# Attention with a mixture of experts: the product with wi in TensorE's two row halves, one step later; first ids ahead of the weights; the third batch's gates earlier

## The chip, the cores and the metric

The kernel runs on one core of a Trainium2 chip. The metric is the device time of one execution in microseconds (us). Each comparison takes the median of several executions. One further execution is profiled: the hardware profiler records every instruction of TensorE (PE, its weight loads as PEld), VectorE (DVE), ScalarE (ACT), GpSimd (POOL) and SyncE (SP, which here issues DMAs), every DMA, and the clock granted to TensorE.

## The reference

Causal attention over 4 batches, 12 heads, 448 positions, 64 elements a head; its output, rows of 12 x 64 = 768 elements, goes through a layer of 8 experts of which each row takes the one with the largest gate logit.

```python
scores = scale * np.matmul(q, k.transpose(0, 1, 3, 2))     # causal mask on top
attn = np.exp(scores - np.max(scores, axis=-1, keepdims=True))
attn = attn / (np.sum(attn, axis=-1, keepdims=True) + 1e-09)
x = np.matmul(attn, v)                                     # then rows of B*S, columns of H*D
...
logits = x @ w_gate
expert_idx = np.argmax(logits, axis=1)
probs = np.exp(logits - logits.max(-1, keepdims=True))
probs /= probs.sum(-1, keepdims=True) + 1e-09
gate_w = probs[np.arange(N), expert_idx]
for e in range(E):
    mask = expert_idx == e
    out[mask] = gate_w[mask, None] * (np.maximum(x[mask] @ w1[e], 0.0) @ w2[e])
```

## The kernel before

**Pairs and steps.** The attention works on 24 pairs of heads (`NP`), six to a batch (`NPB`). The 448 positions are four chunks of 112 (`C`). The order of the instructions on every engine is the order in which the code is written. `step(p)` lays pair p+1's scores beside pair p's transposes and pair p-1's values, and is called for p from -1 to 22; a list written out by hand takes the place of step 23 (the tail).

**One step.** `scores(n, c)` (n = p+1) multiplies chunk c of the queries with the keys up to it, for the pair's two heads, whose 64 elements lie in partitions 0 to 63 and 64 to 127: two matmuls of 64 rows, into two PSUM banks. VectorE masks and takes the row maximum (L137), ScalarE takes exp and its row sum (L141). `transposes(p, j)`, j from 0 to 4, turns four blocks of 112 x 112 each into one PSUM bank (L160); ScalarE copies them to `pt` (L167), but j = 1 is copied by VectorE (L165). `values(p-1, kc)` multiplies by v (L178); its result, transposed, is copied to `xt` by VectorE (L184), which takes the reciprocal row sums `rs` too (L187, L188).

**The product with wi.** `back(p-1, i)` for i = 0 and 1 closes the step: two chunks of `xt` each are the stationary operand, and `wi` the moving one, 128 rows of 144 columns. `wi` holds, for each pair and for each of the two heads, an identity of 64 columns and that head's rows of `w_gate`, 8 columns; the other head's rows are zero. So one product turns x back into rows and gives the head's part of the logits. VectorE scales both by `rs` into `x` (112 x 256) and `lgp` (112 x 32) (L206, twice each per `back`); after i = 1 SyncE writes x to the rows `xd` in DRAM (L211).

**PSUM.** The tag "pst" of the pool `ps_t` has three banks. The five transposes of a step, the two psb tiles of `back`, and now and then the rank's tile take these three in turn; a tile's first matmul waits for the reader of the tile that had the bank before.

**Routing.** After a batch's sixth pair has gone through `back`, `route(b)` is put on the list `todo`. It is a generator: `drip()` runs it up to its next `yield`, one piece after each transposes of a step (from pair 18 on, after each scores too). Its pieces: `choose` (POOL adds the logits' parts up, VectorE finds the maximum and the one-hot choice), ScalarE's exp, `rank` (four matmuls with triangular and all-one matrices count each row's place, L325 and L326, into a bank of "pst"), `places` (row numbers; POOL scatters the rows' numbers into the tables `idtab` in DRAM with four indirect DMAs, L345), and `gates` (the gate's value, written to `xd`, L320). For the third batch (b = 2) `early_slots` comes between places and gates: it finds, from the three batches counted so far, the experts of the first three slots of 128 rows. There SyncE reads slot 0's expert number, issues two loads of raw weights (`load_raw`, L565, 768 KB each), then slot 0's four id columns (`load_ids`, L572, from `idtab`), then two further weight loads. The last four weight loads, POOL's `merge_ids`, and its `gather` of the rows (L586) stand at the end of `route(2)`.

**The tail and the experts.** The tail runs the last pair's transposes and values between the first weights' splits (`split_parts`, ScalarE L622 and VectorE L628) and turns the first gathered slot (`x_turn`, L657); then the slots of the experts run one after another (L697 on).

## Time and profile before

| | us |
|---|---|
| median of three executions | 533.37 (529.67 to 534.95) |
| the profiled execution | 535.47, of which the profile's span is 533.6 |
| TensorE busy in the span | 506.9 (95%) |
| VectorE, ScalarE busy | 308.8 and 309.8 (58% each) |
| POOL busy | 119.5 (22%) |

The attention takes the span's first 206 us, the experts the rest. The page of the profile gives shares of whole runs; the timeline gives each engine's groups of equal instructions with their start, their length and, in brackets, how long the engine sat idle before them and what ended that; a table of windows gives any stretch's busy times and the granted clock, as a share of full speed. A group's length runs from its first start to its last end. A matmul in float32 is recorded as two rows, each with its weight load.

### The profile page before, as it was taken

The numbers are of one execution on the slowest core, as the hardware profiler recorded it, in microseconds if no ns is written. First come the engines' busy times: TensorE is split into PE (matmuls) and PEld (weight loads), VectorE is DVE, ScalarE is ACT, GpSimd is POOL, SyncE is SP. The second block draws the span as 40 slices with busy tenths as digits, with TensorE's granted clock in tenths as the row PEclk, the third lists the DMA queues.
The fourth block names the chain that finished last, engine by engine and source line by source line (L and its number), as shares of the span: only waits on it lengthen the run. The fifth ranks groups of instructions, "written<-read, shape, count | busy, mean of one in ns | idle before, by whom it ended". The sixth has DMA issues, their size and how long they took to land. (4 is left out here: it accounts for less than half of the span.)

```text
span 533.6 us, 10959 instructions
## 1 busy us (share of the span) xinstructions
PE 506.9 (95%) x3114; PEld 408.0 (76%) x3114; DVE 308.8 (58%) x826; ACT 309.8 (58%) x692; POOL 119.5 (22%) x199
## 2 busy tenths in 40 slices
PE   8999999999998898999999999999999999989991
PEld 5666665675675666898899889988998899878871
DVE  4777776776766687731113635648437213795590
ACT  6878767777776674521224636457455424974660
POOL 1000122013014327131120311214323110333213
PEclk9999999999999798999999999999999999999997
DMA  8544425533635759011157486486673169967720
GB/s 208 137 132 133 140 83 87 173 98 116 134 100 101 133 145 380 10 32 33 51 164 281 134 269 215 141 282 216 225 244 121 51 173 316 328 210 248 247 88 17
DMA packets 56537, 85.33 MB, mean 160 GB/s; under 512 B 16906, under 2 KB 28426, under 8 KB 56464
## 3 DMA queue, kind: packets, MB, share of 16 engines
q1 hardware_dynamic: 53072, 73.42, 47.1%
q0 software_dynamic: 3392, 11.08, 5.5%
q8 instruction: 28, 0.46, 0.4%
q14 instruction: 45, 0.37, 0.4%
HBM read 137.68 MB, written 12.88 MB: 282 GB/s over the span
## 5 line engine op out<-in xcount | busy, mean ns | idle before, releaser
L628 DVE TENSOR_TENSOR lo<-raw,hi 128x1536 fp32r<-128x1536 f32 x64 | 110.2, 1755 | 30.8 <-ACT hi L622 21.5
L141 ACT ACTIVATE s<-s,nm 112x112 f32<-112x112 f32 (+1 forms) x192 | 99.2, 518 | 46.6 <-DVE nm L137 43.2
L622 ACT CAST hi<-raw 128x1536 fp32r<-128x1536 f32 x64 | 92.9, 1484 | 10.8 <-PE y L782 7.9
L137 DVE CUSTOM_DVE_ANT_0 s<-ps,cs 112x112 f32<-112x112 f32 (+1 forms) x192 | 75.4, 446 | 21.9 <-PE ps L134 20.3
L697 PE MATMUL l<-hi,xh 128*128 128x512 f32 x216 | 87.3, 404 | 0.0
L686 ACT COPY hs<-l 128x512 f32<-128x512 f32 x36 | 21.1, 586 | 92.6 <-PE l L684 92.4
L787 PE MATMUL y<-lo,hh 128*128 128x384 f32 x280 | 72.7, 341 | 0.1
L702 PE MATMUL l<-lo,xh 128*128 128x512 f32 x180 | 72.0, 400 | 0.6
L782 PE MATMUL y<-hi,hh 128*128 128x384 f32 x250 | 64.6, 340 | 0.4
L134 PE MATMUL ps<-qk 64*112 64x112 f32 (+3 forms) x384 | 60.4, 432 | 0.9 <-DVE nm L137 0.6
L718 DVE SCALAR_TENSOR_TENSOR hl<-hT,hh 128x512 fp32r<-128x512 f32 x28 | 19.3, 689 | 68.2 <-ACT hh L715 38.0
L160 PE MATMUL pst<-cs,s 112*112 112x112 f32 x480 | 57.9, 268 | 0.5 <-ACT pt L167 0.5
L160 PEld LDWEIGHTS pst<-cs,s 112*112 112x112 f32 x480 | 46.9, 136 | 11.7 <-issue 6.4
L178 PE MATMUL psx<-pt,v 112*64 112x448 f32 (+3 forms) x384 | 50.6, 406 | 0.0
L787 PEld LDWEIGHTS y<-lo,hh 128*128 128x128 f32 x280 | 49.8, 189 | 0.4 <-issue 0.4
L178 PEld LDWEIGHTS psx<-pt,v 112*64 112x64 f32 x384 | 25.5, 137 | 30.8 <-issue 20.9
L697 PEld LDWEIGHTS l<-hi,xh 128*128 128x128 f32 x216 | 41.1, 190 | 8.6 <-issue 0.2
L715 ACT ACTIVATE hh<-hT 128x512 fp32r<-128x512 f32 x36 | 21.8, 605 | 43.9 <-PE hT L712 37.8
L167 ACT COPY pt<-pst 112x448 f32<-112x448 f32 x95 | 45.6, 525 | 2.4 <-PE pst L160 2.3
L782 PEld LDWEIGHTS y<-hi,hh 128*128 128x128 f32 x250 | 44.7, 188 | 1.1 <-issue 0.7
L659 DVE TENSOR_TENSOR xl<-xT,xh 128x384 fp32r<-128x384 f32 x36 | 18.4, 553 | 45.8 <-ACT xh L658 45.7
L134 PEld LDWEIGHTS ps<-qk 64*112 64x112 f32 x384 | 28.7, 181 | 19.3 <-issue 9.8
(147 smaller groups left out, 686.5 us busy)
## 6 DMA issues: line engine op xcount, KB each, us to landing
raw<-in_w SPq DMA_DIRECT2D x144, 768.0 KB
qk<-in_qk SPq DMA_DIRECT2D x23, 448.0 KB
v<-in_v SPq DMA_DIRECT2D x24, 224.0 KB
xd<-x SPq DMA_DIRECT2D x24, 224.0 KB
idc<-idtab SPq DMA_DIRECT2D x72, 0.5 KB
qk<-in_qk SPq DMA_DIRECT2D x2, 224.0 KB
wi<-in_wi SPq DMA_DIRECT2D x1, 432.0 KB
xg<-xd,idx POOLq DMA_INDIRECT x18
```

The source lines that it names most:

```text
L134: nc.tensor.matmul(ps[:, :n], t[o, 0, c * C:(c + 1) * C], t[o, 1, :n], start=True, stop=True)
L137: nc.vector.tensor_tensor_reduce(out=s[:, :n], in0=ps[:, :n], in1=cs[:C, O_MASK + S - n:O_MASK + S], scale=-0.125, scalar=3.0e38, op0=ALU. ...
L141: nc.scalar.activation(s[:, :n], s[:, :n], ACTF.Exp, bias=nm[:, h, c:c + 1], scale=-1.0, accum_out=sm[:, c, h:h + 1],)
L160: nc.tensor.transpose(ps[:, i * C:(i + 1) * C], pr_t[p, h, qc][:, kc * C:(kc + 1) * C], ident[:C, :C])
L167: nc.scalar.copy(dst, ps)
L178: nc.tensor.matmul(ps[D * h:D * (h + 1), kc * C:], v[:, kc, h, :], pt[:, o:o + n], start=(kc == 0), stop=(kc == NCH - 1),)
L622: nc.scalar.copy(parts[u][0], flat(u))
L628: nc.vector.tensor_tensor(out=lo, in0=flat(u), in1=hi.bitcast(F32), op=ALU.subtract)
L697: nc.tensor.matmul(ps, xh[:, k], wh[:, i], start=(k == 0), stop=False)
L702: nc.tensor.matmul(ps, xh[:, k], wl[:, i], start=False, stop=False)
L782: nc.tensor.matmul(y_ps[s][d], hi[:, c], wh[:, i, o], start=(h == 0 and c == 0), stop=False)
L787: nc.tensor.matmul(y_ps[s][d], hi[:, c], wl[:, i, o], start=False, stop=(h == 1 and c == 3))
```

## The change

`wi` loses its zeros: 128 x 6 x 72, each head's identity and gate columns in that head's own 64 partitions (216 KB instead of 432). `back(p)` is called once a pair: eight matmuls of 64 rows and 72 columns, head 0's rows and head 1's in turn, into two banks, one for each head. VectorE still runs four instructions, now by head instead of by pair of chunks. In `step(p)` it is called for p-2 instead of p-1, behind `scores(n, 0)` and `scores(n, 1)` and ahead of the transposes. `route(b)` is put on its list right behind that call. For the first three batches `gates` runs ahead of `rank` instead of last. In `early_slots` slot 0's ids come ahead of all eight weight loads.

```diff
-    wi = const.tile([128, NPB, 2 * HW], F32, name="wi")
+    wi = const.tile([128, NPB, HW], F32, name="wi")
...
-    def back(p, i):
+    def back(p):
...
-        ps = ps_t.tile([C, 2, 2 * HW], F32, tag="pst", name="psb")
-        for j in range(2):
-            c = 2 * i + j
-            nc.tensor.matmul(ps[:, j], xt[:, c * C:(c + 1) * C], wi[:, pr], start=True, stop=True)
-        src = ps.rearrange("p c (h w) -> p c h w", w=HW)
-        for dst, lo, n in ((X[p], 0, D), (LG[b][:, :, 2 * pr:2 * pr + 2], D, E)):
-            nc.vector.tensor_tensor(
-                out=dst[:, 2 * i:2 * i + 2], in0=src[:, :, :, lo:lo + n],
-                in1=rs[:, 2 * i:2 * i + 2, :].unsqueeze(3).to_broadcast([C, 2, 2, n]), op=ALU.mult,
-            )
...
+        both = [ps_t.tile([C, NCH, HW], F32, tag="pst", name="psb") for _ in range(2)]
+        for c in range(NCH):
+            for h, ps in enumerate(both):
+                o = slice(D * h, D * (h + 1))
+                nc.tensor.matmul(ps[:, c], xt[o, c * C:(c + 1) * C], wi[o, pr], start=True, stop=True)
+        for h, ps in enumerate(both):
+            for dst, lo, n in ((X[p][:, :, h], 0, D), (LG[b][:, :, 2 * pr + h], D, E)):
+                nc.vector.tensor_tensor(
+                    out=dst, in0=ps[:, :, lo:lo + n],
+                    in1=rs[:, :, h:h + 1].to_broadcast([C, NCH, n]), op=ALU.mult,
+                )
...
         yield
+        if b < B - 1:
+            yield from gates(b)
         yield
         rank(b)
...
-        yield from gates(b)
+        if b == B - 1:
+            yield from gates(b)
         if b == B - 2:
             for i in range(1, EARLY):
                 load_regs(i)
                 load_ids(i)
-            for u in range(4, 8):
-                load_raw(0, u)
...
         pos = [
-            (scores, n, 0), (scores, n, 1), (transposes, p, 0), (transposes, p, 1), (transposes, p, 2), (scores, n, 3),
+            (scores, n, 0), (scores, n, 1), (back, p - 2), (transposes, p, 0), (transposes, p, 1), (transposes, p, 2), (scores, n, 3),
             (scores, n, 2), *((values, p - 1, kc) for kc in range(NCH)), (transposes, p, 3), (transposes, p, 4),
-            (back, p - 1, 0), (back, p - 1, 1),
         ]
         for f, *a in pos:
             f(*a)
+            if f is back and p - 1 > NPB - 1 and (p - 1) % NPB == 0:
+                todo.append(route((p - 2) // NPB))
...
         regs[0] = nc.sync.value_load(tab0[0:1, 0:1], min_val=0, max_val=E - 1), None, None
-        for i in range(2):
-            load_raw(0, i)
         load_regs(0)
         load_ids(0)
-        for i in range(2, 4):
+        for i in range(8):
             load_raw(0, i)
...
-            if p >= 1 and (p - 1) % NPB == NPB - 1:
-                todo.append(route((p - 1) // NPB))
...
         for f, *a in [
-            (transposes, p, 0), (transposes, p, 1), (split_parts, 0, (0,), ("low",)), (transposes, p, 2),
+            (back, p - 2), (transposes, p, 0), (transposes, p, 1), (split_parts, 0, (0,), ("low",)), (transposes, p, 2),
             (split_parts, 0, (1,), ("high",)), *((values, p - 1, kc) for kc in range(NCH)),
-            (transposes, p, 3), (split_parts, 0, (1,), ("low",)), (transposes, p, 4), (back, p - 1, 0), (back, p - 1, 1),
-            *((values, p, kc) for kc in range(NCH)), (x_turn, 0), (back, p, 0), (back, p, 1),
+            (transposes, p, 3), (split_parts, 0, (1,), ("low",)), (transposes, p, 4), (back, p - 1),
+            *((values, p, kc) for kc in range(NCH)), (x_turn, 0), (back, p),
```

The first place is TensorE at the turn from one step to the next, before the change: the four matmuls of `back` (L203), the four of scores (L134), and the first transposes (L160), with the engines that each waits for (the numbers behind a name tell tiles apart).

```order
L203 MATMUL psb_477<-wi_70,xt_460 112x144 [waits DVE_49,Activation_49]
L203 MATMUL psb_477<-wi_70,xt_460 112x144
L203 MATMUL psb_482<-wi_70,xt_460 112x144 [waits Activation_49]
L203 MATMUL psb_482<-wi_70,xt_460 112x144
L134 MATMUL ps_495<-qk_272 112x112 [waits DMAHW5_49]
L134 MATMUL ps_496<-qk_272 112x112
L134 MATMUL ps_505<-qk_272 112x224
L134 MATMUL ps_506<-qk_272 112x224
L160 MATMUL pst_516<-cs_69,s_396 112x112 [waits Activation_49]
```

After the change, the same place: the scores stand where `back` stood, and `back` behind them.

```order
L134 MATMUL ps_487<-qk_272 112x112 [waits DMAHW5_49,DVE_49]
L134 MATMUL ps_488<-qk_272 112x112 [waits DVE_49]
L134 MATMUL ps_497<-qk_272 112x224 [waits DVE_49]
L134 MATMUL ps_498<-qk_272 112x224 [waits DVE_49]
L203 MATMUL psb_508<-wi_70,xt_464 112x72 [waits DVE_49,Activation_49]
L203 MATMUL psb_509<-wi_70,xt_464 112x72 [waits Activation_49]
L203 MATMUL psb_508<-wi_70,xt_464 112x72
L203 MATMUL psb_509<-wi_70,xt_464 112x72
```

What moved: the product with wi has gone from ahead of the scores to behind them, as eight matmuls of half width.

The second place is the next few rows on TensorE before the change: T0's last transposes, then T1 (tile pst_522) and T2 (pst_528).

```order
L160 MATMUL pst_516<-cs_69,s_435 112x112
L160 MATMUL pst_522<-cs_69,s_406 112x112 [waits DVE_49,PE_49]
L160 MATMUL pst_522<-cs_69,s_445 112x112
L160 MATMUL pst_522<-cs_69,s_435 112x112
L160 MATMUL pst_522<-cs_69,s_445 112x112
L160 MATMUL pst_528<-cs_69,s_435 112x112 [waits DVE_49,PE_49]
L160 MATMUL pst_528<-cs_69,s_435 112x112
```

After the change, T1 is tile pst_530 and T2 pst_536.

```order
L160 MATMUL pst_524<-cs_69,s_439 112x112
L160 MATMUL pst_530<-cs_69,s_393 112x112 [waits DVE_49,PE_49]
L160 MATMUL pst_530<-cs_69,s_449 112x112
L160 MATMUL pst_530<-cs_69,s_439 112x112
L160 MATMUL pst_530<-cs_69,s_449 112x112
L160 MATMUL pst_536<-cs_69,s_439 112x112 [waits Activation_49]
L160 MATMUL pst_536<-cs_69,s_439 112x112
```

What moved: T1 waits for VectorE as before, T2 for Activation (ScalarE) where it waited for VectorE; this stands so in every step that has a `back` in it.

The third place is SyncE's queue behind the third batch, before the change: reading slot 0's expert number (L420), raw weights (L565), and slot 0's ids (L572); DMASW is the queue of POOL's scatters.

```order
L420 TENSOR_LOAD tab_112 [waits DVE_49]
L420 ISA x2
L565 ISA
L565 DMA raw_116<-in_w 128x3x512 [waits DMAHW7_49]
L565 ISA
L565 DMA raw_117<-in_w 128x3x512 [waits DMAHW0_49]
L532 TENSOR_LOAD tab_112 [waits DVE_49]
L532 ISA x2
L572 REGISTER_ALU
L572 DMA idc<-idtab_73 128x1 [waits DMAHW1_49,DMASW0_49]
L572 REGISTER_ALU
L572 DMA idc<-idtab_74 128x1 [waits DMAHW2_49,DMASW1_49]
```

After the change, the gates' row (L322) stands ahead of them, and the ids ahead of the weights.

```order
L322 DMA xd<-pre 112x4x8 [waits DMAHW6_49,DVE_49]
L210 DMA xd<-x 112x4x128 [waits DMAHW7_49,DVE_49]
L422 TENSOR_LOAD tab_112 [waits DVE_49]
L422 ISA x2
L532 TENSOR_LOAD tab_112 [waits DVE_49]
L532 ISA x2
L572 REGISTER_ALU
L572 DMA idc<-idtab_73 128x1 [waits DMAHW0_49,DMASW0_49]
L572 REGISTER_ALU
L572 DMA idc<-idtab_74 128x1 [waits DMAHW1_49,DMASW1_49]
L572 REGISTER_ALU
L572 DMA idc<-idtab_75 128x1 [waits DMAHW2_49,DMASW2_49]
```

What moved: `pre` has gone from behind the ids and four of the weights to the front, and the weights from both sides of the ids to behind them.

## Rows read from the trace of the kernel before

**Rows 1.** TensorE's steps in windows: length, busy time (instructions) of each engine, PEclk, DMA share, GB/s
```profile
68.68:86.29 17.61, 16.01 (x126) 10.64 (x125) 11.90 (x54) 12.31 (x41) 5.50 (x12) 1.00 0.36 104
101.53:109.15 7.62, 7.62 (x61) 5.08 (x61) 5.63 (x26) 6.06 (x20) 0.00 (x0) 1.00 0.45 120
116.77:134.27 17.50, 16.01 (x126) 10.63 (x125) 12.09 (x54) 12.32 (x41) 5.40 (x12) 1.00 0.39 106
157.23:186.77 29.54, 26.41 (x185) 17.98 (x184) 20.35 (x101) 18.50 (x61) 11.41 (x41) 0.88 0.66 117
```

**Rows 2.** Timeline of one undisturbed step: start us, us, engine, line, operation, xcount
```profile
101.15 0.42 DVE L206 TENSOR_TENSOR x<-psb,rs 112x256 f32<-112x256 f32 x1 [0.58 <-PE psb L203]
101.49 0.18 DVE L206 TENSOR_TENSOR lgp<-psb,rs 112x32 f32<-112x32 f32 x1
...
101.53 0.83 PE L134 MATMUL ps<-qk 64*112 64x112 f32 x8
...
102.12 0.28 DVE L137 CUSTOM_DVE_ANT_0 s<-ps,cs 112x112 f32<-112x112 f32 x1
...
102.29 1.36 PE L160 MATMUL pst<-cs,s 112*112 112x112 f32 x12
...
102.44 0.39 ACT L141 ACTIVATE s<-s,nm 112x112 f32<-112x112 f32 x1 [1.34 <-DVE nm L137]
...
103.14 0.08 DVE L137 DVE_READ_ACCUMULATOR2_ANT nm<- 112x1 f32 x1
...
103.58 1.57 PE L134 MATMUL ps<-qk 64*112 64x448 f32 x8
...
104.13 0.94 ACT L167 COPY pt<-pst 112x448 f32<-112x448 f32 x2
...
108.02 1.21 PE L203 MATMUL psb<-wi,xt 128*112 128x144 f32 x8
```

**Rows 3.** Timeline of TensorE in the first batch's rank; idle time before and its releaser in brackets
```profile
71.30 0.36 PE L325 MATMUL rank<-base,cs 112*112 112x40 f32 x2 [0.49 <-DVE pt L165]
71.49 0.36 PE L326 MATMUL rank<-oh,cs 112*112 112x32 f32 x2
71.78 0.63 PE L134 MATMUL ps<-qk 64*112 64x448 f32 x2
```

**Rows 4.** Timeline of TensorE, first two score multiplies of the undisturbed step alone
```profile
101.53 0.45 PE L134 MATMUL ps<-qk 64*112 64x112 f32 x4
```

**Rows 5.** Timeline of TensorE at three waits: step 1, first and third batch's transitions
```profile
14.47 0.80 PE L134 MATMUL ps<-qk 64*112 64x112 f32 x7 [0.33 <-DMA qk<-in_qk]
...
85.15 0.71 PE L203 MATMUL psb<-wi,xt 128*112 128x144 f32 x4 [0.87 <-DVE rs L187]
...
175.04 2.23 PE L203 MATMUL psb<-wi,xt 128*112 128x144 f32 x8 [2.40 <-DVE rs L187]
```

**Rows 6.** Windows behind two stalls, columns as in group 1
```profile
175.04:182.00 6.96, 6.96 (x32) 5.44 (x34) 4.42 (x25) 3.32 (x12) 1.68 (x10) 0.54 0.93 139
205.90:209.20 3.30, 3.30 (x11) 2.73 (x11) 2.80 (x6) 3.30 (x3) 2.32 (x2) 0.57 1.01 387
```

**Rows 7.** Timeline of SyncE's DMA issues behind the third batch
```profile
170.61 1.45 SPq L565 DMA_DIRECT2D raw<-in_w  x2
175.91 9.65 SPq L572 DMA_DIRECT2D idc<-idtab  x4
185.76 0.96 SPq L565 DMA_DIRECT2D raw<-in_w  x2
...
187.34 1.59 SPq L320 DMA_DIRECT2D xd<-pre  x1
```

**Rows 8.** Timeline of GpSimd (POOL): last scatter, and the first slot's gather
```profile
170.17 0.93 POOL L345 DMA_INDIRECT idtab<-ids_c,rowi  x1 [0.30 <-issue]
...
197.27 1.38 POOL L586 DMA_INDIRECT xg<-xd,idx  x1 [7.87 <-DMA idc<-idtab]
```

**Rows 9.** Timeline of TensorE at the first expert's transposes
```profile
203.76 0.87 PE L657 MATMUL xT<-cs,xg 128*128 128x128 f32 x6 [1.67 <-DMA xg<-xd,idx]
```

More of the change, by code (lines that the diff above doesn't have):

```diff
@@ L193, in back @@
         b, pr = divmod(p, NPB)
-        if i == 0:
-            X[p] = x_p.tile([C, NCH, 2, D], F32, name="x")
-            if pr == 0:
-                LG[b] = small.tile([C, NCH, H, E], F32, tag="lgp", name="lgp")
+        X[p] = x_p.tile([C, NCH, 2, D], F32, name="x")
+        if pr == 0:
+            LG[b] = small.tile([C, NCH, H, E], F32, tag="lgp", name="lgp")
         xt = xts_t[p]
         rs = st[p][2]
-        ps = ps_t.tile([C, 2, 2 * HW], F32, tag="pst", name="psb")
-        for j in range(2):
-            c = 2 * i + j
-            nc.tensor.matmul(ps[:, j], xt[:, c * C:(c + 1) * C], wi[:, pr], start=True, stop=True)
-        src = ps.rearrange("p c (h w) -> p c h w", w=HW)
-        for dst, lo, n in ((X[p], 0, D), (LG[b][:, :, 2 * pr:2 * pr + 2], D, E)):
-            nc.vector.tensor_tensor(
-                out=dst[:, 2 * i:2 * i + 2], in0=src[:, :, :, lo:lo + n],
-                in1=rs[:, 2 * i:2 * i + 2, :].unsqueeze(3).to_broadcast([C, 2, 2, n]), op=ALU.mult,
-            )
-        if i == 1:
-            nc.sync.dma_start(
-                xd[b * S:(b + 1) * S, 128 * pr:128 * (pr + 1)].rearrange("(c p) f -> p c f", p=C),
-                X[p].rearrange("p c h d -> p c (h d)"),
-            )
+        both = [ps_t.tile([C, NCH, HW], F32, tag="pst", name="psb") for _ in range(2)]
[9 more added lines that the diff above has]
+                )
+        nc.sync.dma_start(
+            xd[b * S:(b + 1) * S, 128 * pr:128 * (pr + 1)].rearrange("(c p) f -> p c f", p=C),
+            X[p].rearrange("p c h d -> p c (h d)"),
+        )
     todo = []
@@ L317, in gates @@
         V.tensor_scalar_add(g["sm"], g["sm"], 1e-9)
-        yield
+        if b == B - 1:
+            yield
         V.reciprocal(g["pre"], g["sm"].unsqueeze(2).to_broadcast([C, NCH, E]))
@@ L990, in layout @@
     vv = v.reshape(NP, 2, NCH, C, D).transpose(0, 3, 2, 1, 4)
-    wi = np.zeros((128, NPB, 2 * HW), np.float32)
+    wi = np.zeros((128, NPB, HW), np.float32)
     g = moe_w_gate.reshape(NPB, 2, D, E)
     for h in range(2):
-        wi[h * D:(h + 1) * D, :, h * HW:h * HW + D] = np.eye(D, dtype=np.float32)[:, None, :]
-        wi[h * D:(h + 1) * D, :, h * HW + D:(h + 1) * HW] = g[:, h].transpose(1, 0, 2)
+        wi[h * D:(h + 1) * D, :, :D] = np.eye(D, dtype=np.float32)[:, None, :]
+        wi[h * D:(h + 1) * D, :, D:] = g[:, h].transpose(1, 0, 2)
     return {
```

## The prediction

> **What bounds the kernel now.** I read the profile's busy table first: TensorE is busy almost all the time, so the question is only where it waits and how long each step of the attention takes. Then I cut the span into windows, each step from its first score multiply (scores, S) to the next one's [rows 1]: an undisturbed step takes 7.62 us and TensorE is busy for all of it. Two steps after a batch end take 17.61 and 17.50 us instead of 15.24, the three steps after the third batch 29.54 instead of 22.86. These extras, 2.37 + 2.26 + 6.68 = 11.3 us, together with a stall before the mixture of experts, are what a reordering can win. The mixture of experts behind them is untouched by the diff.
>
> Next comes the timeline of one undisturbed step [rows 2]. Read it as one ring: first scores S0+S1 at 101.53, first three transposes T0 to T2 at 102.29, last scores S3, S2 at 103.58, values, T3 and T4, then the product with wi (B) at 108.02; the next S0 at 109.15 ends the window. So S0 to S3 is 2.05 us, S3 to B 4.44, B to S0 1.13; the sum is 7.62.
>
> **Ring of the transposes: the change's price.** B leaves its place, so S0 stands where B stood, 4.44 us behind S3 (4.45, since a turn from full to half rows lies there either way). B now lies between S1 and T0. Its 144 columns become 72, its rows 64, and two halves are to run side by side. No row shows that form. Bounds: the score rows have halves side by side with 112 weight columns, and rank, with only 40 and 32 moving columns, still starts two passes every 0.19 us [rows 3], so 0.095 a pass. Below, half of B's column time, 8 x 0.06 = 0.5; above, sixteen passes one after another, 16 x 0.095 = 1.5. I take 8 x 0.095 = 0.77, since the rank rows are nearest.
>
> What decides is not that figure. B now takes two of the three PSUM banks at the step's front, and the order shows what T1 and T2 then wait for: T1 the VectorE's reading of B's first half, T2 Activation, whose latest instruction of that kind is its copy of T0. Before, both waited for VectorE alone, which was long done. That T2 takes over T0's bank follows from that wait: B's halves and T1 are read by VectorE. Behind T2 stands all of TensorE's queue, and ScalarE's later exps wait for S3. The scores' own new wait for VectorE costs nothing: B in the same place waited for VectorE's later sums.
>
> Worked out from S0's start as 0, with durations of [rows 2]. S0 ends at 0.45 [rows 4]; the max starts at 0.49 (no evacuation of B before it on VectorE any more); the first exp 0.32 later, as 102.12 to 102.44; the four exps take 104.13 - 102.44 = 1.69, so the copy of T0 starts at 2.50. Two copies take 0.94, so one is over 0.5 later, at 3.00, and T2 starts at 3.05. T0 to S3 took 1.29, that is twelve passes of 0.095 and 0.15 around; T2 to S3 is then four passes and 0.15, 0.53. S3 starts at 3.58 instead of 2.05. The step is 3.58 + 4.45 = 8.03 us, 0.41 longer. T1's wait is swallowed in it: the four maxes end at 0.49 + 1.10, x and lgp of the first half follow in 0.34 + 0.18, so T1 starts at about 2.3. With that wait alone S3 would start at 2.3 + 8 x 0.095 + 0.15 = 3.21 and the step be 7.66.
>
> Bounds: if the copy of T0 comes as late as it does now (104.13 + 0.5 is 3.10 behind S0), the step is 8.13; if T2 is not held, 7.66. I take 8.03: the order shows the wait and the chain of exps is a row. It holds in the 21 steps that have a B and scores: 21 x 0.41 = **+8.6 us**. ScalarE's busy time is 6.06 and VectorE's 5.63 of a step [rows 1]: not their sum but the place in the queue holds T2.
>
> The Trainium skill, "TensorEngine Tiling (Array Packing)", section "Performance Considerations", says that tiling speeds up TensorE but not the evacuation of PSUM, which may become the bottleneck. Taken as a sum of evacuation, that rule would cost nothing here, 6.06 being under 7.62; taken as a wait for one copy it is the 8.6 us.
>
> **Start and end of the ring.** The step that had a B first loses it (-1.13), and the wait of 0.33 for qk behind the larger wi falls [rows 5]: **-1.45**. The last product comes into the tail instead: 0.77 and two turns of rows of about 0.1: **+1.0**. Two further products in the tail are cheaper, 8 x (0.121 - 0.095) each, where 0.121 is B's step from 108.02 to 109.15 less 0.16 around it, over eight: **-0.4**.
>
> **Transitions of batches one and two.** Of their extras, rank itself is 0.48 from its first pass to S3 and VectorE wakes it late by 0.49 [rows 3]; B waits 0.87 for a reciprocal sum while the indirect scatters run [rows 5]. Moved between transposes, rank costs four passes, 0.4, without its wait. B is no longer where the scatters land, but other TensorE instructions are; between nothing and 0.87 of that wait, and what the choosing chain takes from VectorE, I take 0.6. So 1.0 a transition, 2.0 instead of 4.63: **-2.6**. The gates moved ahead of rank are three small VectorE instructions, hidden by VectorE's idle 2 us a step.
>
> **Third batch.** B waits 2.40 us, until 175.04 [rows 5]; from there 6.96 us run at a granted clock of 0.54 [rows 6], the lower of the two levels for nearly all of it, 6.96 x 0.46 = 3.2 us lost, and the rest are rank and its wait. Two weight loads are issued at 170.61, right behind the last scatter at 170.17, and run beside the wait [rows 7, 8]. Now no weight is issued before the ids, which wait for the scatters. I take half of the 2.40, no fall of the clock, and rank: 1.6 instead of 6.68: **-5.1**.
>
> **First gather.** SyncE issues the first slot's ids from 175.91, for 9.65 us, and the gates' rows only at 187.34, behind raw weights [rows 7]; the gather on POOL comes at 197.27 after 7.87 us of waiting, and TensorE waits 1.67 us for its rows at 203.76 [rows 8, 9]; then 3.30 us run at 0.57, costing 1.4 [rows 6]. With gates and ids ahead, the gather is issued at about 190 (197.27 less its wait is 189.4) and, at the present 6.5 us from 197.27 to 203.76, lands by 196.5, six before it is needed: **-1.67** and **-1.4**. Its cover: these six us. Of the weights, third and fourth are issued behind the ids at 185.76 already now [rows 7]; the first two move in front of them there, so each comes two loads later, hidden by the 18 us up to 203.76. If that cover went, ScalarE's split and the first expert multiply would wait for them.
>
> **Sum:** 8.6 - 1.45 + 1.0 - 0.4 - 2.6 - 5.1 - 1.67 - 1.4 = -3.0 us. The profiled execution took 535.47 (its span of 533.6 and 1.9 around it), so 532.4; the runs shown have their median 2.1 lower, 533.37, so **530.4**.
>
> **Rivals.**
> *Third batch's stall stays* (whatever instruction stands there waits, and the clock falls after it): the other 1.2 and 3.2 come back, 534.8. For it: the wait is put on a reciprocal that should be long done, so its cause isn't seen. Against: weights no longer run there, and transitions without weights waited 0.87.
> *The gather is still late* (scatters land late, ids too): 1.67 + 1.4 back, 533.5. Against: six us of cover.
> *T2 is not held*: step 7.66, 21 x 0.37 = 7.8 less, 522.6. For it: only an order, no trace, shows the wait. Against: that order, and exps which cannot come earlier.
> *Slower: the clock falls in the lengthened steps.* TensorE would idle about 0.7 us in every one of 21 steps. Both falls in the rows came behind an idle stretch, of 2.40 and 1.67. A fall costs 3.2 or 1.4; from three of the larger kind the change is slower, 530.4 + 9.6 = 540.0. Against: transition steps with waits of 0.87, and 0.49 together with others, kept a clock of 1.00 [rows 1].
> *Slower: the halves don't run side by side*, so the change doesn't do what it says: B takes 1.5, T0 comes 0.77 later and is done at 2.8, its copy at 3.35, S3 starts at 3.93, the step is 8.38: 21 x 0.35 = 7.4 and three products in the tail 2.3 more, 540.1. Against: S3 and S2 in halves take 1.57 for eight rows of 448 and 336 columns; at B's 0.121 per 144 columns one after another they would take 2.6.
> The Trainium skill, "TensorE: Matmul & The Clock Gate", section "LDWEIGHTS (loading the stationary operand)", says that a weight load takes its columns over 1.2 ns, whatever its rows: an estimate of 93 ns for 112 columns, by which halving the rows wins nothing unless both halves load at once. The trace agrees on the 93 (0.095 in rank), and the score rows show loads at once.
>
> **How the numbers follow.** Forecast 0.47, third batch's stall 0.20, late gather 0.13, T2 not held 0.10, clock falls 0.06, halves in turn 0.04. Forecast's own range: half a unit of each taken middle, 527 to 533. From 524.5 to 537.5 leaves out the last three, 0.20. About 1% is what a measurement tells from no change, 528.0 to 538.7: faster are T2 not held and the lower third of the forecast, 0.10 + 0.17; slower the last two, less what they share with a gain, 0.08; the rest, 0.65, is within.
>
> **What would show it.** Step cut as above at 8.0; waits of T1 for VectorE and of T2 for ScalarE's copy, some 0.3 to 0.4 each, in 21 steps; S3 at 3.6 behind S0; B of 0.8 behind S1; TensorE's clock 1.00 behind the third batch's last product, gather issued before 192, no wait of the first expert's transposes. It is wrong if steps stay near 7.6, if a stall of over 2 us stands behind the third batch, or if the clock leaves 1.00 inside the steps.

## The result, and the profile after

The changed kernel takes 539.04 us (median of 4, 538.27 to 539.83) against 532.54 us of the kernel before, measured beside it: 1.011 times the time, 95% interval 1.006 to 1.016. Repeated on another chip it took 536.35 against 529.92, 1.0155 (1.009 to 1.022). It is slower; 530.4 had been forecast, with 537.5 as the range's upper end.

The first view is the windows of the profile after, cut as in [rows 1] at each step's first score multiply: the first batch's transition, an undisturbed step, the second batch's transition, the three steps behind the third batch, the last of these alone, the stretch from there to the first expert's multiply, and the rest.

```profile
70.24:86.76 16.52, 15.66 (x141) 10.37 (x141) 11.79 (x54) 12.55 (x42) 5.81 (x13) 1.00 0.51 89
103.04:111.18 8.14, 7.65 (x69) 5.01 (x69) 5.54 (x25) 6.16 (x21) 0.00 (x0) 1.00 0.66 209
119.31:135.84 16.53, 15.67 (x141) 10.37 (x141) 11.85 (x54) 12.56 (x42) 5.63 (x13) 1.00 0.51 90
160.26:189.32 29.06, 25.67 (x209) 16.11 (x208) 19.39 (x98) 18.08 (x59) 8.31 (x25) 0.94 0.23 52
177.59:189.32 11.73, 9.78 (x69) 5.72 (x68) 6.72 (x39) 5.63 (x18) 1.99 (x8) 0.85 0.16 6
189.32:209.97 20.65, 19.27 (x175) 13.30 (x174) 15.27 (x48) 13.87 (x34) 4.60 (x20) 1.00 0.93 334
209.97:536.40 326.43, 308.99 (x1652) 276.52 (x1650) 162.74 (x202) 158.40 (x205) 87.36 (x113) 0.99 0.52 172
```

An undisturbed step is 8.14 us instead of 7.62. The timeline of one such step shows where (columns as in [rows 2]):

```profile
103.04 0.83 PE L134 MATMUL ps<-qk 64*112 64x112 f32 x8
103.63 0.27 DVE L137 CUSTOM_DVE_ANT_0 s<-ps,cs 112x112 f32<-112x112 f32 x1 [0.45 <-PE ps L134]
103.70 0.92 PE L203 MATMUL psb<-wi,xt 64*112 64x72 f32 x16
103.95 0.39 ACT L141 ACTIVATE s<-s,nm 112x112 f32<-112x112 f32 x1 [0.22 <-DVE nm L137]
...
104.55 0.59 PE L160 MATMUL pst<-cs,s 112*112 112x112 f32 x4
...
105.32 0.56 PE L160 MATMUL pst<-cs,s 112*112 112x112 f32 x4 [0.18 <-DVE lgp L206]
...
105.64 0.51 ACT L167 COPY pt<-pst 112x448 f32<-112x448 f32 x1
...
106.20 0.60 PE L160 MATMUL pst<-cs,s 112*112 112x112 f32 x4 [0.31 <-ACT pt L167]
```

The product runs in 0.85 us, from 103.70 to T0 at 104.55, so its halves do lie side by side. Then T1 waits for VectorE's `lgp` and T2 for ScalarE's copy of T0, which starts at 105.64 behind the four exps. T2 starts 3.16 us behind S0. The two waits, 0.18 and 0.31 us, are nearly all of the 0.52 us that the step has gained; TensorE's busy time in it is 7.65 us against 7.62. The table of waits sums over the whole run (us in total, times, longest); the single row below them is before's, where the first wait was 0.5 us in one instance and the second was not there:

```profile
PE pst L160 <- ACT pt L167: 6.9, 22, 0.5
PE pst L160 <- DVE lgp L206: 3.8, 19, 0.7
PE xT L657 <- DMA xg<-xd,idx: 2.7, 2, 1.7
```

```profile
PE pst L160 <- ACT pt L167: 0.5, 1, 0.5
```

The first slot's gather is now in time, but the second slot's is not. The timelines of SyncE, POOL and TensorE behind the third batch; [rows 7 to 9] answer to them:

```profile
180.85 6.39 SPq L572 DMA_DIRECT2D idc<-idtab  x4
187.43 7.65 SPq L565 DMA_DIRECT2D raw<-in_w  x8
195.18 1.13 SPq L210 DMA_DIRECT2D xd<-x  x1
198.28 12.48 SPq L572 DMA_DIRECT2D idc<-idtab  x8
```

```profile
194.59 1.13 POOL L586 DMA_INDIRECT xg<-xd,idx  x1 [0.77 <-POOL idx L581]
211.10 4.84 POOL L580 TENSOR_TENSOR idc<-idc 128x2 int32<-128x2 int32 x1 [15.38 <-DMA idc<-idtab]
```

```profile
220.65 0.52 PE L657 MATMUL xT<-cs,xg 128*128 128x128 f32 x3 [1.68 <-DMA xg<-xd,idx]
```

Gather of slot 0 at 194.59 instead of 197.27, and no wait at its transposes. But the eight id columns of slots 1 and 2 (198.28, for 12.48 us) stand behind eight weight loads, POOL waits 15.38 us for them, and TensorE waits 1.68 us at slot 1: the 1.67 us of [rows 9], one slot later.

The two profiled executions by stretches, in us (after less before; the forecast beside it):

| stretch | forecast | measured | how |
|---|---|---|---|
| start, to S0 of step 2 | -1.45 | -1.55 | 21.41 against 22.96 |
| 21 steps | +8.6 | +10.9 | 21 x (8.14 - 7.62) |
| batches one and two, extra over plain steps | -2.6 | -4.1 | 0.24 + 0.25 left of 4.63 |
| third batch, extra over three plain steps | -5.1 | -2.0 | 29.06 - 3 x 8.14 = 4.64 left of 6.68 |
| last step to first expert | -1.1 | +0.5 | 20.65 - 19.62 - 0.52 counted above |
| experts | -1.4 | -0.8 | 326.43 - 327.23 |
| sum | -3.0 | +2.9 | spans 536.4 and 533.6: +2.8 |

The medians differ by 6.5, not 2.8: the profiled execution of before (535.47) lies above all four that its median is taken from (529.67 to 534.95), that of after is the lowest of its four.

### The profile page after: what moved, and what is told of

The parts are those of the page before. It is cut to its first block, busy times and chain, and to the rows that moved or that the text cites. A ratio compares the mean times of both kernels' runs of the same rounds, so it can differ in the third digit from the quotient of the medians.

```text
span 536.4 us, 11338 instructions
## 1 busy us (share of the span) xinstructions
PE 503.0 (94%) x3306; PEld 402.7 (75%) x3306; DVE 306.2 (57%) x826; ACT 312.3 (58%) x692; POOL 116.5 (22%) x199
## 5 line engine op out<-in xcount | busy, mean ns | idle before, releaser
L137 DVE CUSTOM_DVE_ANT_0 s<-ps,cs 112x112 f32<-112x112 f32 (+1 forms) x192 | 75.1, 445 | 35.9 <-PE ps L134 32.8
L160 PE MATMUL pst<-cs,s 112*112 112x112 f32 x480 | 65.2, 267 | 11.9 <-ACT pt L167 6.9
L702 PE MATMUL l<-lo,xh 128*128 128x512 f32 x180 | 70.8, 394 | 0.6
L160 PEld LDWEIGHTS pst<-cs,s 112*112 112x112 f32 x480 | 45.7, 134 | 26.9 <-ACT pt L167 12.1
L134 PE MATMUL ps<-qk 64*112 64x112 f32 (+3 forms) x384 | 59.8, 429 | 1.4 <-DMA qk<-in_qk 1.4
L167 ACT COPY pt<-pst 112x448 f32<-112x448 f32 x95 | 47.9, 527 | 18.8 <-PE pst L160 16.2
L659 DVE TENSOR_TENSOR xl<-xT,xh 128x384 fp32r<-128x384 f32 x36 | 18.4, 552 | 44.0 <-ACT xh L658 43.8
L134 PEld LDWEIGHTS ps<-qk 64*112 64x112 f32 x384 | 27.8, 176 | 19.7 <-issue 10.0
```

Source lines behind the costliest of these rows:

```text
L134: nc.tensor.matmul(ps[:, :n], t[o, 0, c * C:(c + 1) * C], t[o, 1, :n], start=True, stop=True)
L137: nc.vector.tensor_tensor_reduce(out=s[:, :n], in0=ps[:, :n], in1=cs[:C, O_MASK + S - n:O_MASK + S], scale=-0.125, scalar=3.0e38, op0=ALU. ...
L160: nc.tensor.transpose(ps[:, i * C:(i + 1) * C], pr_t[p, h, qc][:, kc * C:(kc + 1) * C], ident[:C, :C])
L167: nc.scalar.copy(dst, ps)
L702: nc.tensor.matmul(ps, xh[:, k], wl[:, i], start=False, stop=False)
```

## The experiments

Each time stands beside the kernel before in the same job, since the jobs ran on several chips, on which the kernel before has medians from 529.87 to 533.87 us.

**Is the wait for T0's copy the price?** The last of the four exps goes behind that copy.

```diff
+            late = c == 1 and h == 1 and 1 < p < NP
+            (owed_exp.append if late else lambda f: f())(lambda s=s, h=h: nc.scalar.activation(
...
-            (back, p - 2), (transposes, p, 0), (transposes, p, 1), ...
+            (back, p - 2), (transposes, p, 0), (exp_owed,), (transposes, p, 1), ...
```

> The changed kernel, with the last of the four exps of the first two score blocks issued behind ScalarE's copy of T0. Theory: T2 then starts about 0.45 us earlier (copy at 2.1 instead of 2.6 behind S0) and the step is about 7.7 us instead of 8.14; 21 x 0.45 = 9 us less than the changed kernel, about 530. Rival (T0's copy is not what T2 waits for, or the exp then delays something else as much): steps stay above 8.0, 537 or more.

532.16 against 533.87 of before: 0.9967 (0.994 to 0.999). The timeline of TensorE in one step (the edit adds lines, so transposes are L162 here):

```profile
108.01 0.83 PE L135 MATMUL ps<-qk 64*112 64x112 f32 x8
108.68 0.92 PE L205 MATMUL psb<-wi,xt 64*112 64x72 f32 x16
109.53 0.59 PE L162 MATMUL pst<-cs,s 112*112 112x112 f32 x4
110.30 1.10 PE L162 MATMUL pst<-cs,s 112*112 112x112 f32 x8 [0.17 <-DVE lgp L208]
111.32 1.57 PE L135 MATMUL ps<-qk 64*112 64x448 f32 x8
```

T1 and T2 now run as one group, T2's wait is gone, and the step is 7.77 us instead of 8.14. One exp moved wins back 0.37 of the 0.52 us, so the forecast's mechanism is shown. T1's wait stays: from T0 to T1 it is 0.77 us, where four passes are 0.38, so it costs 0.39. That the whole time comes out below that of before has further reasons: in this run step 21 takes 10.23 us instead of 11.73, and slot 1 does not wait.

**Is it the halves or their place?** Before, with the product in halves where the product had been.

```diff
-            (back, p - 1, 0), (back, p - 1, 1),
+            (back, p - 1),
```

> Before, with one part of the change alone: wi of half size and the product in two row halves, but at its old place, for the pair before, behind T4. Theory (the ring's wait, not the halves, costs the time): the product falls from 1.13 us to about 0.8, nothing waits for T0's copy, and a step takes 7.3 us instead of 7.62; over 23 products some 6 to 8 us less than before, about 525. Rival (two banks at once make T1 or T2 wait at this place too): steps of 7.6 or more, no gain.

536.67 against 533.87: 1.0055 (1.002 to 1.009). Steps of 7.60: no gain. The timeline at the end of a step:

```profile
106.61 0.97 ACT L167 COPY pt<-pst 112x448 f32<-112x448 f32 x2
...
106.89 1.21 PE L203 MATMUL psb<-wi,xt 64*112 64x72 f32 x15
...
107.85 0.29 PE L134 MATMUL ps<-qk 64*112 64x112 f32 x1
```

The product still takes 1.09 us, from 106.89 until S0 goes on at 107.98, against 0.85 in the changed kernel. The likely reason is that its second half takes over T3's bank: T3's copy, started at 106.61, is half done when the first half starts. The profile marks no wait in this step; in a later one (142.29) it marks 0.57 us for ScalarE's copy behind the product's first two passes. So two banks at once seem to cost a wait at this place too, where I had expected 0.3 us less; the rival of that run was the right one, though with the product's own second half as the one that waits. The equal steps do not explain why the median is 2.8 us above that of before: the profiled execution, 533.75, is the lowest of the ten, and it stays open where the others lose.

**Which of the third batch's costs are the program's?** Without its scatters:

```diff
-        for c in range(NCH):
+        for c in range(NCH if b != B - 2 else 0):
```

> The changed kernel without the third batch's four indirect scatters: that batch's row numbers are not written to the tables, so its rows reach no expert. Theory (the stall in the second step behind the third batch comes from the scatters, during which TensorE's signals reach the other engines late): that step falls from 11.73 to 8.2 to 8.5 us, the clock stays at 1.00 behind it, the step before keeps its rank and T1's wait (9.2); 2.5 to 3.5 us less in all. Rival (it comes from the slots' choice on VectorE and SyncE's reading of it): a wait of over 1 us stays there and the step stays above 10.

The second step behind the batch fell from 11.73 to 8.29, the clock stayed at 1.00:

```profile
177.59:185.88 8.29, 7.66 (x69) 5.02 (x69) 7.06 (x40) 6.27 (x21) 1.75 (x10) 1.00 0.34 95
```

Other kernels on that chip, with their scatters, have the stall (3.10 us with the routing parts alone, a step 21 of 12.66 in the reordered kernel; both below). That spoke for the scatters, by one execution without them. Then the weights were put back around the ids as before the change:

```diff
+        for i in range(2):
+            load_raw(0, i)
         load_regs(0)
         load_ids(0)
-        for i in range(8):
+        for i in range(2, 4):
             load_raw(0, i)
```

> The changed kernel with the weights ordered around the ids as before the change: two loads, the first slot's ids, two loads, and four behind the ids of slots 1 and 2; gates stay early. Theory (the first gather waited for the ids and the gates' rows, both slowed by the weights): with gates early alone the ids still land late beside two weight loads; the first slot's transposes wait 1 to 2 us again, 537 to 539. Rival (the gates' rows, issued behind weights, were what made it late): no wait at the first slot, none at slot 1, 535 to 536.5 as with ids ahead of the weights.

532.75 against 529.87: 1.0083 (1.005 to 1.012), and the step was 8.29 with the scatters in place. Neither of the first two slots waited for its gather, which is the rival's sign; but the rival's reason, the early gates, is not shown by it. The first gather was issued no earlier than before (197.27 in [rows 8]):

```profile
197.24 2.81 POOL L590 DMA_INDIRECT xg<-xd,idx  x1 [0.77 <-DMA raw<-in_w]
```

Its rows landed 5.7 us later, at about 202.9, and TensorE came to slot 0's transposes only at 203.61. In the third profile of before (below), where the attention ends sooner, TensorE was there at 194.35 and waited 3.80 us for a gather issued at 193.36. So the longer steps hid this gather, and what early gates are worth alone is not shown; ids ahead of the weights do bring it forward, on one chip from 197.37 to 190.07. For the stall, this run was on another chip, and its absence had no reason in the program. So four kernels went to one chip together: the changed one, this one, the one without scatters, and the kernel before.

> The changed kernel again, on one chip with the next three. If the stall is the program's: step 21 takes 11 to 12 us again and the time is 1% above before. If it is the chip's or the execution's: step 21 may take 8.3 us, and the time then lies some 3 to 4 us lower against before, within 0.5% of it.

> The changed kernel with the weights ordered around the ids as before, again. If the order of SyncE's loads decides the stall: step 21 takes 8.3 us here and 11.7 in the changed kernel on the same chip, and this kernel is 4 us or more faster than that. If chip or execution decide: both alike, and this kernel is faster by slot 1's 1.7 us alone.

> The kernel before, a third profile. If the stall is the program's: 2.4 us at the product with wi in step 20 again, step 20 above 10.5 us. If it is the chip's or the execution's: it differs from the two profiles so far, as the changed kernel's does on this chip.

> The changed kernel without the third batch's scatters, again. Theory (without scatters no stall, on any chip): step 21 takes 8.1 to 8.4 us. Rival (the first profile of it was by chance without one): step 21 above 10.

On that chip no kernel has the stall. Steps 20 and 21 take 9.20 and 8.29 in the changed kernel, 9.20 and 8.30 in the one with the old order of weights, 9.21 and 8.29 without scatters; in the kernel before they take 7.62 and 7.66, behind a rank step of 8.83, and the extra step behind batches one and two is not there either. The third profile of before (530.20) thus has only its rank waits and, at the first expert, a wait of 3.80 us for the gather. The second profile of before, on a chip with the stall:

> The kernel before, unchanged, for a second profile. Theory: the profiled execution of before (535.47) lay high among its runs (529.67 to 534.95), so the third batch's stall of 2.40 us or the 6.96 us at the lower clock behind it are not there every time; then the stretch of three steps behind the third batch is shorter than 29.54 us, by up to 3 us. Rival: both are there in every execution, and the stretch is 29.5 again, the total about 535.

537.56, with 10.61 for the step at 2.45 us of wait and 3.04 at the first gather. What the stall is can be read from VectorE's first max (L137) of that step, in the changed kernel on the first chip and on the later one; S0 started at 177.59 and at 177.43:

```profile
179.87 0.27 DVE L137 CUSTOM_DVE_ANT_0 s<-ps,cs 112x112 f32<-112x112 f32 x1 [1.64 <-PE psb L203]
```

```profile
177.93 0.26 DVE L137 CUSTOM_DVE_ANT_0 s<-ps,cs 112x112 f32<-112x112 f32 x1
```

2.28 us behind S0's start against 0.50, at the same place of the program, with the last scatter issued 0.28 us after S0's start in both (177.87 and 177.71): while scatters run, VectorE takes up TensorE's results late on some chips and not on others. I call these late signals; the rows show VectorE idle for 1.64 us behind multiplies that were over (S0's first two end 0.45 us behind its start), and not what holds it up. One reordered kernel (below) shows the same once more, with the identical program on two chips:

```profile
162.94:170.24 7.30, 7.30 (x70) 4.87 (x69) 6.98 (x38) 6.14 (x21) 3.60 (x5) 1.00 0.05 3
```

```profile
162.48:176.18 13.70, 10.56 (x69) 6.22 (x69) 7.30 (x39) 6.39 (x21) 3.61 (x5) 0.75 0.09 4
```

Both are step 21, which the scatters reach. Over all runs, five profiles with scatters come from two chips, and none has the stall; eight, with scatters beside S0 to T2 or beside the old product, come from three other chips, and all have it. The executions that were not profiled agree: on the two chips the kernel before has medians of 529.87 and 529.92, on the three 533.16 to 533.87. On the chip of the four kernels, old and new order of weights differ by 532.61 to 536.35: 3.7 us, of which the profiles show 1.63 at slot 1.

**Weights four to seven behind the ids of slots 1 and 2**, the rest as in the changed kernel:

> The changed kernel, with the last four of the first expert's eight weight loads put back behind the ids of slots 1 and 2. Theory (the gather's stall moved from slot 0 to slot 1, because those ids queue behind eight loads of 768 KB): the wait of 1.68 us at slot 1's transposes goes, and nothing comes instead; about 1.5 us less than the changed kernel, 537.5. Rival (slot 1's ids are late by the scatters or the chain on POOL): the wait stays at 1.5 or more.

536.33 against 533.87: 1.0064 (1.003 to 1.010). The wait at slot 1 is gone (its transposes, L659 in this kernel, are not among the waits up to there), and nothing came in its place: ids behind 768 KB loads were its cause. They cost only where the chain is late: in the run with one exp moved the same ids stand behind the same eight loads, go out 6.4 us earlier (191.90) and slot 1 does not wait.

**Does the place in the step matter?** The third batch's route goes on behind scores only from step 21 on, so that rank stands between T3 and T4 of step 20.

```diff
-            if f is transposes or f is scores and p >= NP - NPB:
+            if f is transposes or f is scores and p >= NP - 3:
```

> The changed kernel with the third batch's route stepped on behind scores only from step 21 on, instead of 18; rank then stands between transposes late in step 20, as for the first two batches, and the scatters run while the values are multiplied, not beside S0 to T2. Theory (what the scatters cost is decided by where in the step they fall): the two steps behind take 8.5 and 8.1 to 8.4 instead of 9.20 and 11.73, the clock stays at 1.00, and the first gather comes some 6 us later, at about 200, still in time; 3 to 4 us less than the changed kernel, 535 to 536. Rival (they stall whatever runs beside them, or the first gather is late again): less than 1.5 us less.

540.64 against 533.16: 1.013 (1.006 to 1.021). The steps fell as the theory said, to 8.49 and 8.03, on a chip whose other kernels have the stall. The time did not fall all the same (the changed kernel had 1.011), since the chain is later by some 5 us (slot 0's ids go out at 185.71 instead of 180.85) and slot 1's ids still stand behind eight loads:

```profile
221.61 1.51 PE L657 MATMUL xT<-cs,xg 128*128 128x128 f32 x6 [5.45 <-DMA xg<-xd,idx]
```

With both mended together:

> The changed kernel with both losses of its routing undone: the third batch's route stepped on behind scores only from step 21 on, and the last four weight loads behind the ids of slots 1 and 2; the steps of 8.14 stay. Theory (ring's wait aside, the forecast failed by the third batch's stall and by slot 1's gather): 4 to 5 us of stall and clock and 1.7 us of gather go, 539.0 becomes 532 to 534. Rival (with the route later, slot 1's gather is late whatever stands behind the ids): a wait of 2 us or more at slot 1, 535 or more.

536.76 against 533.57: 1.006 (1.0035 to 1.009); the rival's number, but not by the rival's wait. Slot 1 does not wait. Now ScalarE waits for the first weights, and T3's copy behind it on that engine:

```profile
197.57 1.47 ACT L624 CAST hi<-raw 128x1536 fp32r<-128x1536 f32 x1 [3.30 <-DMA raw<-in_w]
198.95 0.96 ACT L167 COPY pt<-pst 112x448 f32<-112x448 f32 x2
```

```profile
199.53 0.98 PE L160 MATMUL pst<-cs,s 112*112 112x112 f32 x8 [1.07 <-ACT pt L167]
```

That is the cover that the prediction named for the weights; I had counted 18 us of it to the first expert, but the first reader, ScalarE's split, stands in the tail.

**The routing parts alone**, on the kernel before:

> Before, with the routing parts alone: gates early, the first slot's ids ahead of the weights (with the last four weight loads left behind the ids of slots 1 and 2); the product as it was, at its old place. Theory: the first gather is in time, so the stall of 1.7 to 3 us before the first expert and the lower clock behind it go, while the wait of 2.4 us behind the third batch stays though no weights run beside it (the scatters are its cause); about 2 to 4 us less than before, 530 to 532. Rival A (the two weight loads beside the scatters were the cause of the 2.4 us): that wait falls below 1 us too, 5 or more less, under 529. Rival B: no gain, the stall moves to slot 1 or the weights are late.

532.04 against 533.16: 0.9975 (0.994 to 1.001), not to be told from no change. The wait at the first slot is gone, and no lower clock follows it. The product's wait behind the third batch is 3.10 us without any weights beside it, so weights are not its cause:

```profile
175.91 1.44 PE L203 MATMUL psb<-wi,xt 128*112 128x144 f32 x8 [3.10 <-DVE rs L187]
```

**A reordered version.** Banks in strict turn (T2 then takes the product's second half's bank), S3 between the product and T0, S3's exps behind T0's copy, weights four to seven behind the ids of slots 1 and 2:

```diff
+    def pst(shape, name):
+        return ps_t.tile(shape, F32, tag=f"pst{next(turns) % 3}", name=name)
...
+            (scores, n, 0), (scores, n, 1), (back, p - 2), (scores, n, 3), (transposes, p, 0), (exp_owed,), (transposes, p, 1), (transposes, p, 2),
+            (scores, n, 2), ...
```

> The changed kernel with what the runs point to: the three banks of the transposes in strict turn (T2 then takes over the bank of the product's second half, not T0's), S3 moved between the product and T0 so that VectorE has time to empty the first half, S3's exps behind ScalarE's copy of T0, and the last four weight loads behind the ids of slots 1 and 2. Theory: neither T1 nor T2 waits, the step is 7.3 to 7.4 us, 0.25 less than before and 0.75 less than the changed kernel; the stalls of the third batch stay; 525 to 528. Rival (a wait comes elsewhere, at S3 for the scores' banks or at T0 for ScalarE): steps of 7.6 or more, 531 or more.

522.46 against 533.16: 0.980 (0.973 to 0.988). Steps of 7.29 us, without a wait:

```profile
103.07 0.83 PE L134 MATMUL ps<-qk 64*112 64x112 f32 x8
103.74 0.92 PE L214 MATMUL psb<-wi,xt 64*112 64x72 f32 x16
104.49 0.95 PE L134 MATMUL ps<-qk 64*112 64x448 f32 x4
105.37 1.36 PE L171 MATMUL pst<-cs,s 112*112 112x112 f32 x12
106.67 0.82 PE L134 MATMUL ps<-qk 64*112 64x336 f32 x4
```

S3's 0.88 us stand between the product and T0, and in them VectorE empties the banks. The run makes these changes together; what each is worth is not separated. Its steps 20 and 21 kept 2.3 and 5.4 us of extra, so the route was moved in it too, to step 21 and to step 20, and the latter once with two weight loads ahead of the ids:

> The reordered kernel (S3 ahead of T0, banks in strict turn) with the third batch's route stepped on behind scores only from step 21 on. Theory (the place of rank and of the scatters in the step makes the 7.7 us of extra time in steps 20 and 21, which the reordered kernel still has): these steps fall from 9.62 and 12.65 to 7.6 to 7.9 us, no lower clock behind them, and with half of the weights behind the ids slot 1's gather stays in time; 5 to 7 us less than the reordered kernel, 516 to 518. Rival (the chain comes 6 us later, so the first or second slot's gather is late): steps as said, but a wait of 2 us or more at a slot's transposes, 519 to 522.

> The reordered kernel with the third batch's route stepped on behind scores from step 20 on, between its two forms run so far (18 and 21): rank stands behind T0 of step 20, and ids and weights come some 4 us earlier than in the late form. Theory (early form pays at rank and in the scatters' shadow, late form at ScalarE, whose first split waits 4.0 us for the first weights and holds back T3's copy): less of both, 518 to 521. Rival (the scatters' shadow falls on the next step's first scores again): step 21 over 9.5 us and the lower clock behind it, 522 or more.

> The reordered kernel e11 again, for the comparison on one chip: 1.5 to 2% faster than before, steps of 7.29, the tail's two waits of about 1 us at T3 and the product.

> The reordered kernel (route stepped on behind scores from step 20 on) with two weight loads ahead of the first slot's ids again, as before the change. Theory (the tail's waits of 1.2 and 1.0 us at T3 and the product come from weights that stand behind the ids): both go, and the first gather, with the gates early, is still in time; 1.5 to 2.5 us less than the next kernel on the same chip. Rival (the first gather is late again, by the ids): a wait of 1 to 4 us at the first slot's transposes, no gain or a loss.

524.97 against 533.57, 0.983 (0.979 to 0.988); 519.75 against 529.87, 0.987 (0.978 to 0.995), and on another chip 524.05 against 533.55, 0.985 (0.980 to 0.990); 521.66 against the same 533.55, 0.983 (0.977 to 0.988). None can be told from the others. In the first the steps fell as said (7.64 and 7.86), and the tail paid, by ScalarE's wait of 4.0 us for the first weights; in the second, on a chip without the stall, by 1.2 and 1.0 us; on the chip with the stall the tail did not wait, since the attention itself ended later, so whether two loads ahead of the ids are worth something could not be seen there.

## Why the prediction was wrong

*The ring.* The mechanism was the right one, and its place: T2 waits for T0's copy in each step. The term was 0.41 a step and measured 0.52. Of its chain the first link was off: the max was to start 0.04 us behind S0's end, since no evacuation stood before it on VectorE any more, and starts 0.14 behind it (103.63 less 103.04 and the 0.45 of [rows 4]). That is 0.59 behind S0's start, as before (102.12 less 101.53 in [rows 2]); where VectorE had been evacuating, it now sits idle until TensorE's scores come. From there all durations held: exp 0.32 later, copy 1.69 later, T2 0.56 later, S3 0.53 later, the rest 4.45. Over 21 steps: 2.3 us. The Trainium skill, "TensorEngine Tiling (Array Packing)", section "Performance Considerations", says that tiling speeds up TensorE but not the evacuation of PSUM, whose copy may become the bottleneck. The trace agrees as to a wait for evacuation, 10.9 us over the steps, and not as to its amount: the sums of ScalarE's and VectorE's work (6.16 and 5.54 of 8.14) stay below the step.

*Third batch, 5.1 us, measured 2.0.* This step failed most. The stall was there in the one execution that was read, and I took it for a property of the kernel and laid half of it on the two weight loads; in the run with the routing parts alone the product waits 3.10 us with no weights beside it. On a chip without late signals the kernel before has nothing to win there, and in the changed kernel, where there are late signals, they came back at the next place that has no slack: S0 to T2 of step 21, 11.73 us with 3.40 us at the lower clock. The rival "third batch's stall stays" was the likelier; I had given it 0.20, having noted myself that the cause wasn't seen. Rank, too, came to stand at a place I had not looked up for the third batch: since its route also steps on behind scores, between S1 and the product, where T1 then waits 0.70 and step 20 takes 9.19, not between transposes.

*Gather, 1.67 and 1.4.* The wait at slot 0 went, as forecast, but in part by luck: behind the stall the gather was issued at 194.59, not before 192, and TensorE came for it at 207.37, where before it had come at 202.09 (203.76 less the wait). The step that failed is "its cover": I asked only who needs the weights that move behind the ids, not whose ids stand behind the eight weights. Slots 1 and 2 have eight id columns there, and slot 1 pays 1.68.

*Batches one and two, 2.6.* Too little: 0.24 and 0.25 were left instead of 1.0 each. Rank between T3 and T4 costs 0.35, its wait is gone, and the late signals fell beside the values: the copy to `xt` starts 7.71 us behind S0 (86.44) against 7.24 on the chip without them, and TensorE waits for neither. On that chip before has no second long step, and the term is 2.3.

*Tail.* Products there were to be cheaper by 0.2 each. They are not: the three take 1.25, 1.62 and 1.84, the two of before 1.39 and 1.92, so they cost 1.4 more instead of 0.6; no row gave the 0.1 taken for a turn of rows. In the second of the three TensorE waits 0.28 us for a copy of ScalarE's (L167) behind the first two passes, as in the run with halves at the old place. Step 22, behind the stall, takes 8.67 us to its end, 0.5 more than a plain one.

*The median.* I subtracted 2.1 us to go from the profiled execution to the median, and still took gains from the very stalls that made that execution slow. On the chip without late signals the two profiles differ, by stretches, by -1.3 us to S0 of step 2 (21.26 against 22.58); +8.0 over the next twenty steps, which is 10.4 for the plain steps less 2.3 for the first two batches (two steps of 9.02 before; 8.49 and 8.03 twice now), the third batch giving nothing (1.25 extra before, 1.21 now); -2.0 from the last step to the first expert, where the wait of 3.80 is gone; and -0.5 in the experts, where 1.63 came at slot 1. That is +4.2, the difference of the spans of 528.3 and 532.5. The medians there differ by 6.4; the profiled execution of the changed kernel is again the lowest of its four.

The rivals on the clock and on halves in turn fell: the clock stays at 1.00 in the lengthened steps, and the product takes 0.85 for 16 half passes, so two at a time.

## What to carry to other kernels

Before a product is split over more banks of a small ring, follow for each later tile of the ring which reader frees its bank and what stands ahead of that reader in its engine's queue: here one copy behind four exps cost 0.5 us a step, and one block of independent work put in between, with the banks in strict turn, turned 1% lost into 1.3 to 2% won. Before a stall is counted as a gain, look whether a second execution, on another chip, has it at all. When one load is moved ahead in a queue, list everybody who is now behind it, up to the next reader of each.

## What the runs showed of the hardware

While POOL's four indirect scatters run, VectorE takes up TensorE's results late on some chips (first max 2.28 us behind S0's start) and not on others (0.50), with the same program at the same place; it costs only where the step has no slack. Without the scatters the step was short in both executions that were profiled, one of them on a chip whose other kernels have the stall. Behind such a stall the granted clock fell to the lower level, 0.54 over 3.40 us, as the windows show:

```profile
183.20:186.60 3.40, 3.40 (x12) 1.21 (x12) 0.64 (x4) 0.53 (x1) 0.00 (x0) 0.54 0.07 5
```

What differs between those chips stays open; no run here could show it.
